# A ScalarE Square with its scale in an engine register, and q's transposes copied by ScalarE instead of VectorE

## The chip, the cores and the metric

The kernel runs on one core of one Trainium2 chip. The metric is the device time of one execution in microseconds (us). Five engines of the core matter here: TensorE (PE in the profile, its weight loads PEld), VectorE (DVE), ScalarE (ACT), GpSimd (POOL) and SyncE (SP), which issues all the DMAs. Each engine executes its own queue in order and waits for the others by semaphores.

## The reference

Two stages. First an attention through 49 agents, for 2 batches of 12480 tokens of width 128; then a feed-forward layer of width 2048 whose activation is a rational function.

```
a2k = softmax(scale * agents @ k.T);  agent_v = a2k @ v          # 49 x 128 per batch
q2a = softmax(scale * q @ agents.T);  x = q2a @ agent_v          # 24960 x 128
h = x @ w_in                                                     # 24960 x 2048
P = a0 + a1*h + a2*h^2 + a3*h^3
Q = 1 + |b0|*|h| + |b1|*h^2
out = (P / (Q + 1e-6)) @ w_out                                   # 24960 x 128
```

## The kernel before

The matrix `agent_v` (49 x 128) is multiplied by `w_in` once per batch, so that h comes directly from the softmax weights of q: h = q2a @ M with M = agent_v @ w_in. M is kept as two parts in fp32r, `m_hi` and `m_lo`.

**Tiling.** Tokens go in 49 blocks of 512; w_in's columns in 16 chunks of 128. A block times a chunk is a 128 x 512 tile of h, and three such tiles in a row make a unit: 784 tiles, 262 units. A unit's h stands in PSUM in one of two slots of three banks. The loop of `main` (lines 595 to 630) makes a step per unit. In step i the engines get, in this order in their queues:

- ACT, `act(i)`: the Square of unit i (line 545, `x = (h + xb)^2`), then, for a pair of earlier units, in turn a Ln (line 559) or an Exp with factor -1 (line 561), which together give 1/Q; then what other streams have put on hold for ACT (`run_hold`).
- DVE: `dve2(i)` (line 574, `w = max(h, mu) + x`, from which the Ln makes the denominator's logarithm), `dve1(i)` (line 566, `u = (x + kap) * h`, over x), its hold list, and for every fourth unit `dve_last` (line 579, `u = (u + om) * w`, for the unit six steps back).
- POOL: for the other three of four units the same product in two instructions: `u = u + om` (line 617) and, six steps later, `u = u * w` (line 612).
- PE, `mm1(i + 1)` (lines 480 and 481: three tiles of h, two matmuls each), `mm2(i - 7)` (line 488: the product with w_out, 16 chunks added up in one of two banks `outb`), and then one piece of another stream (`attend`), which uses the `outb` bank that mm2 doesn't use at the time.

A slot of h is read by the Square, dve2 and dve1, and is free for the unit after next when all three have finished. So every engine's queue order and the two slots together set the pace.

**Streams beside the loop.** `q_stream` makes the softmax of q for every second block: scores (line 209), maximum and difference (408, 409), Exp (413), sum and reciprocal (418, 419), the split in two fp32r parts on POOL (426 to 428), then two sets of four PE transposes (line 433, `q_tr`) and for each set a copy of the 113 x 512 result from PSUM to the tile `pT` (line 439, `q_trev`), which mm1 reads as its moving operand. `a2k_stream` computes batch 1's agent attention in the first half of the loop, `w_stream` decodes the rest of w_out at its start.

**Coefficients.** `coefs` (lines 309 to 387) turns a and b into about forty per-partition columns of the tile `cf`, by small DVE and POOL instructions in the opening stage, before the loop. h is scaled by `rho` so that the formulas above hold; a flag chooses between the loop described here and a slower general one. The prologue (lines 718 to 842) is batch 0's agent attention.

Of the kernel before, what the change touches and what calls it, by code (L numbers as in the profile page):

```python
# [11 lines left out]
F32 = mybir.dt.float32  # L12
F32R = mybir.dt.float32r
I32 = mybir.dt.int32
U32 = mybir.dt.uint32
AF = mybir.ActivationFunctionType
# [6 lines left out]
A = 49  # L23
# [24 lines left out]

MAX_G, MAX_A, MAX_K, MAX_C = 16.0, 8.0, 1e9, 1e3

GAP, LAG = 6, 7

ON_DVE, LAST_DVE = 4, 7
# [9 lines left out]
SUBS = (0, 1, 2, 3)  # L63
SUB_DVE = 5

CO0, COPS = 3, 3
QPE, QTR = 2, 7

WARM, DUM, DUA = 8, 2, 4
# [9 lines left out]
def agent_attention_rational_moe(  # L79
# [24 lines left out]
    ag = const.tile([128, B * A], F32, name="ag")  # L104
    cab = const.tile([128, 6], F32, name="cab")
    b_abs = const.tile([128, 2], F32, name="b_abs")
    cf = const.tile([128, 64], F32, name="cf")
    mcol = const.tile([128, 1], F32, name="mcol")
    flag = const.tile([128, 1], I32, name="flag")
    c0_t = const.tile([128, 1], F32, name="c0_t")  # L110
# [198 lines left out]
    def coefs():  # L309

        ops, at = [], {}

        def later(f, **kw):
            ops.append(lambda: f(**kw))

        def new(nm):
            if nm not in co:
                co[nm] = cf[:, len(co):len(co) + 1]
            return co[nm]

        def ts(nm, x, s1, op0, s2=None, op1=None, eng=DVE):
            kw = {} if op1 is None else {"op1": op1}
            later(eng.tensor_scalar, out=new(nm), in0=x, scalar1=s1, scalar2=s2, op0=op0, **kw)

        def tp(nm, x, s1, op0, s2=1.0, op1=ALU.mult):
            ts(nm, x, s1, op0, s2, op1, POOL)


        big = ("km", "cm", "om", "A0", "K", "rho", "mu")
        for nm in big + tuple(nm + "_" for nm in big):  # L330
            new(nm)
        sizes, signed = cf[:, len(big):2 * len(big)], cf[:, :len(big)]

        mul, add = ALU.mult, ALU.add
        ge, le = ALU.is_ge, ALU.is_le
        mag, fit, safe = (sm_p.tile([128, 6], F32, name=n) for n in ("mag", "fit", "safe"))
        later(DVE.scalar_tensor_tensor, out=mag, in0=cab, scalar=-1.0, in1=cab, op0=mul, op1=ALU.max)
        later(DVE.tensor_scalar, out=fit, in0=mag, scalar1=MAX_C, scalar2=None, op0=le)
        later(DVE.scalar_tensor_tensor, out=fit[:, 3:6], in0=mag[:, 3:6], scalar=1.0 / MAX_C, in1=fit[:, 3:6], op0=ge, op1=mul)
        later(DVE.tensor_reduce, out=new("fits"), in_=fit, axis=AX.X, op=ALU.min)  # L340
        ts("unfit", co["fits"], -1.0, mul, 1.0, add)
        later(DVE.tensor_scalar, out=b_abs, in0=mag[:, 4:6], scalar1=1.0, scalar2=None, op0=mul)
        later(DVE.tensor_scalar, out=safe, in0=cab, scalar1=co["fits"], scalar2=co["unfit"], op0=mul, op1=add)
        later(DVE.tensor_scalar, out=mag, in0=mag, scalar1=co["fits"], scalar2=co["unfit"], op0=mul, op1=add)
        a0, a1, a2, a3 = (safe[:, i:i + 1] for i in range(4))
        b0, b1 = mag[:, 4:5], mag[:, 5:6]
        later(DVE.reciprocal, out=new("r3"), in_=a3)
        later(DVE.reciprocal, out=new("rb0"), in_=b0)
        ts("pos", a2, a3, mul, 0.0, ALU.is_gt)
        ts("sig", co["pos"], -2.0, mul, 1.0, add)  # L350
        tp("bb", b1, co["rb0"], mul, 0.5, mul)
        tp("rho", co["bb"], co["sig"], mul)
        tp("t2", co["rho"], co["r3"], mul)
        tp("A2", a2, co["t2"], mul)
        tp("t1", co["t2"], co["rho"], mul)
        tp("A1", a1, co["t1"], mul)
        tp("t0", co["t1"], co["rho"], mul)
        tp("A0", a0, co["t0"], mul)
        tp("mu", co["A2"], 1.0, mul, 0.5, add)
        tp("c", co["mu"], 0.5, mul, co["A1"], add)  # L360
        tp("kap", co["c"], 1.0, mul, -0.0625, add)
        tp("cm", co["c"], co["mu"], mul)
        tp("om", co["cm"], -1.0, mul, co["A0"], add)
        tp("ig", co["bb"], co["rb0"], mul, 0.5, mul)
        tp("xb", co["mu"], -1.0, mul, -0.25, add)
        tp("mg", co["mu"], 1.0, mul, 0.0625, add)
        tp("lb", co["ig"], C0, mul, co["mg"], ALU.subtract)
        tp("km", co["kap"], co["mu"], mul)
        at["late"] = len(ops)
        later(DVE.reciprocal, out=new("G"), in_=co["ig"])  # L370
        later(DVE.reciprocal, out=new("K"), in_=co["t0"])
        tp("Kg", co["K"], co["ig"], mul)
        later(DVE.scalar_tensor_tensor, out=sizes, in0=signed, scalar=-1.0, in1=signed, op0=mul, op1=ALU.max)
        ts("mu_G", co["mu_"], co["G"], mul)
        ts("ok0", co["mu_G"], MAX_G, le, co["fits"], mul)
        ts("ok1", co["G"], 4 * MAX_G, le, co["ok0"], mul)
        ts("sum", co["km_"], co["cm_"], add, co["om_"], add)
        ts("A0_m", co["A0_"], MAX_A, mul, -0.0625, add)
        ts("ok2", co["sum"], co["A0_m"], le, co["ok1"], mul)
        ts("ok3", co["K_"], MAX_K, le, co["ok2"], mul)  # L380
        ts("ok4", co["rho_"], 1.0 / MAX_C, ge, co["ok3"], mul)
        ts("ok5", co["rho_"], MAX_C, le, co["ok4"], mul)
        later(DVE.tensor_copy, out=flag, in_=co["ok5"])
        ts("bad", co["ok5"], -1.0, mul, 1.0, add)
        ts("rho_s", co["rho"], co["ok5"], mul, co["bad"], add)
        later(DVE.tensor_scalar, out=mcol, in0=ident[:, A:A + 1], scalar1=co["mu"], scalar2=co["ok5"], op0=mul, op1=mul)
        return ops, at["late"]


# [59 lines left out]
    def main(wk, streams, fast):  # L449
# [91 lines left out]
        def act(i):  # L541
            if i < NU:
                h, w, x, y = slot(i), view("w", i), view("x", i), view("u", i)
                if fast:
                    ACT.activation(out=x, in_=h, func=AF.Square, bias=co["xb"])  # L545
                else:
                    ACT.activation(out=x, in_=h, func=AF.Abs)
                    ACT.activation(out=y, in_=h, func=AF.Identity, scale=cab[:, 3:4], bias=cab[:, 2:3])
                    POOL.tensor_scalar(out=w, in0=x, scalar1=b_abs[:, 1:2], scalar2=b_abs[:, 0:1], op0=ALU.mult, op1=ALU.add)
            if fast:  # L550
                p = (i - 3) // 2
                ready = pair(p) if 0 <= p and 2 * p < NU else []
                ln, ex = i % 2 == 1, i % 2 == 0
            else:
                ready = [view("w", i - 1)] if 0 <= i - 1 < NU else []
                ln = ex = True
            for r in ready:
                if ln:
                    ACT.activation(out=r, in_=r, func=AF.Ln, bias=arm["lb"])  # L559
                if ex:  # L560
                    ACT.activation(out=r, in_=r, func=AF.Exp, scale=-1.0)  # L561

        def dve1(i):
            h, x, y = slot(i), view("x", i), view("u", i)
            if fast:
                DVE.scalar_tensor_tensor(out=y, in0=x, scalar=co["kap"], in1=h, op0=ALU.add, op1=ALU.mult)  # L566
            else:
                DVE.tensor_tensor(out=y, in0=h, in1=y, op=ALU.mult)
                DVE.scalar_tensor_tensor(out=y, in0=y, scalar=cab[:, 1:2], in1=h, op0=ALU.add, op1=ALU.mult)

        def dve2(i):
            h, x, w = slot(i), view("x", i), view("w", i)
            if fast:
                DVE.scalar_tensor_tensor(out=w, in0=h, scalar=co["mu"], in1=x, op0=ALU.max, op1=ALU.add)  # L574
            else:
                DVE.tensor_tensor(out=w, in0=w, in1=x, op=ALU.mult)

# [55 lines left out]
    def q_stream(g0):  # L633
        for g in range(g0, NQ):
            yield (g, None, None)
            yield (None, lambda bk: q_pe(g, bk), [("DVE", lambda bk: q_ev(g, bk))])
            if g + 1 < NQ:
                load_q(g + 1)
            yield (None, None, [("ACT", lambda bk: q_exp(g))])
            yield (None, None, [("DVE", lambda bk: q_sum(g))])  # L640
            yield (None, None, [("POOL", lambda bk: q_split(g)[0]())])
            yield (None, None, [("POOL", lambda bk, j=j: q_split(g)[j]()) for j in (1, 2)])
            yield (None, None, [])
            yield ("late", lambda bk: q_tr(g, 0, bk), [("DVE", lambda bk: q_trev(g, 0, bk, DVE.tensor_copy))])
            if q_n(g) > 4:
                yield ("late", lambda bk: q_tr(g, 1, bk), [("DVE", lambda bk: q_trev(g, 1, bk, DVE.tensor_copy))])

    def w_scale(h):
        w = wo.rearrange("p a b -> p (a b)")[:, h * WP:(h + 1) * WP]
# [64 lines left out]
    with tc.manual_schedule():  # L714
# [136 lines left out]
        def rest(fast):  # L851
# [3 lines left out]
            for n, r in rings.items():  # L855
                r[1] = turns.get(n, 0)
            if fast:
                arm.update(om=co["om"], lb=co["lb"])
            else:
                arm.update(om=cab[:, 0:1], lb=c0_t)  # L860
            main(wk, [q_stream(1), w_stream(fast), a2k_stream(kv, 1, G1)], fast)
# [42 lines left out]
```

## Time and profile before

| | |
|---|---|
| three runs | 1279.61, 1290.75, 1291.05 us; median 1290.75 us |
| profiled execution | 1280.74 us; span 1278.9 us, 1.84 us lie around the span |
| granted TensorE clock over the span | 0.994 |
| PE busy | 1214.2 us (95%) |
| DVE busy | 1211.8 us (95%) |
| ACT busy | 1161.1 us (91%) |
| POOL busy | 1151.9 us (90%) |
| Square (line 545) | 262 instructions, 402.2 us |
| copies of q's transposes on DVE (line 439) | 47 instructions, 32.0 us |

A busy time counts each moment once, although the records of successive instructions on one engine overlap a little: an instruction's record ends when its writes are done, and the next one starts a little before. So what an instruction takes from its engine's time is the distance from its start to the start of the next one where that one follows at once, and this is shorter than its record. PE's busy time holds modelled ends and isn't a measure of how much room PE has. The loop begins 66 us after the start of the span; until about 600 us batch 1's attention runs beside it.

### The profile page before, as it was taken

To read this page: it belongs to the slowest core of one execution; us is meant where nothing else is said; L and a number is where in the kernel's file an instruction comes from. 1 tells how busy PE (TensorE), PEld (TensorE's weight loads), DVE (VectorE), ACT (ScalarE), POOL (GpSimd) and SP (SyncE) were. 2 spreads that over 40 slices of the span, in tenths; PEclk is the share of its full clock that TensorE was granted. 3 is DMA by queue.
4 is the path that set the end of the run, shared out by engine and by line. 5 is a ranking of instruction groups with operands and counts; after the bars stand their busy time and mean duration, and the time that the engine had idled before them with its cause. 6 is when DMAs were issued, how large, how long until landed. Compare 5 with 4: busy or idle time off the path is not lost.

```text
span 1278.9 us, 14253 instructions
## 1 busy us (share of the span) xinstructions
PE 1214.2 (95%) x5396; PEld 700.8 (55%) x5396; DVE 1211.8 (95%) x941; ACT 1161.1 (91%) x705; POOL 1151.9 (90%) x535
## 2 busy tenths in 40 slices
PE   7969999999999999999999999999999999999998
PEld 6745555555555555555555555555555555555554
DVE  5899999999999999999999999999999999999996
ACT  3478998999999999999999999999999999999995
POOL 3549999989999999999999999999999999999992
PEclk8999999999999999999999999999999999999999
DMA  9511111111011211210000000000000000000000
GB/s 360 201 45 33 42 59 50 42 58 46 34 42 46 62 50 50 58 38 9 33 9 25 34 24 9 34 25 12 30 25 17 25 26 9 33 15 9 17 9 26
DMA packets 22397, 56.60 MB, mean 44 GB/s; under 512 B 2736, under 2 KB 3248, under 8 KB 22320
## 3 DMA queue, kind: packets, MB, share of 16 engines
q1 hardware_dynamic: 22320, 55.61, 12.8%
q8 instruction: 44, 0.72, 0.2%
q14 instruction: 33, 0.27, 0.1%
HBM read 42.82 MB, written 12.78 MB: 43 GB/s over the span
## 4 chain that ended last, share of the span: by engine, by line
DVE 42%; PE 26%; POOL 15%; ACT 8%; issue 8%; DMA 1%; SPq 0%; POOLq 0%; DVEq 0%; ACTq 0%
DVE w L574 17%; DVE u L566 16%; PE outb L488 14%; POOL u L612 8%; POOL u L617 5%; ACT u L545 5%; PE slot L480 4%; PE slot L481 4%; DVE u L579 2%; ACT w L559 2%; PE outb L209 1%; ACT w L561 1%; DVE pT L439 1%; PE outb L433 1%; DVE qs L418 1%
## 5 line engine op out<-in xcount | busy, mean ns | idle before, releaser
L488 PE MATMUL outb<-u,wo 128*128 128x512 f32 (+1 forms) x1568 | 716.7, 593 | 19.8 <-POOL u L612 13.3
L612 POOL TENSOR_TENSOR u<-u,w 128x1536 f32<-128x1536 f32 x192 | 689.4, 3603 | 0.0
L574 DVE SCALAR_TENSOR_TENSOR w<-slot,cf,u 128x1536 f32<-128x1536 f32 (+1 forms) x262 | 471.0, 1798 | 25.5 <-ACT u L545 23.7
L566 DVE SCALAR_TENSOR_TENSOR u<-u,cf,slot 128x1536 f32<-128x1536 f32 (+1 forms) x262 | 472.3, 1803 | 9.3
L488 PEld LDWEIGHTS outb<-u,wo 128*128 128x128 f32 x1568 | 292.1, 189 | 308.3 <-issue 242.1
L545 ACT ACTIVATE u<-slot,cf 128x1536 f32<-128x1536 f32 (+1 forms) x262 | 402.2, 1536 | 62.0 <-PE slot L481 28.1
L617 POOL TENSOR_SCALAR u<-u,cf 128x1536 f32<-128x1536 f32 x192 | 368.3, 1920 | 59.1 <-DVE u L566 58.8
L480 PE MATMUL slot<-pT,m_hi 113*128 113x512 f32 (+3 forms) x800 | 362.7, 455 | 21.5 <-DVE u L566 21.4
L559 ACT ACTIVATE w<-w,cf 128x3072 f32<-128x3072 f32 (+1 forms) x134 | 373.2, 2788 | 0.0
L561 ACT ACTIVATE w<-w 128x3072 f32<-128x3072 f32 (+1 forms) x134 | 361.0, 2696 | 0.0
L481 PE MATMUL slot<-pT,m_lo 113*128 113x512 f32 (+3 forms) x800 | 311.4, 390 | 0.0
L480 PEld LDWEIGHTS slot<-pT,m_hi 113*128 113x128 f32 x800 | 150.3, 188 | 108.5 <-DVE u L566 64.1
L481 PEld LDWEIGHTS slot<-pT,m_lo 113*128 113x128 f32 x800 | 151.0, 189 | 42.8 <-issue 17.8
L579 DVE SCALAR_TENSOR_TENSOR u<-u,cf,w 128x1536 f32<-128x1536 f32 (+1 forms) x70 | 142.3, 2039 | 0.0
L433 PEld LDWEIGHTS outb<-ident,p 128*113 128x113 f32 x187 | 26.4, 178 | 28.3 <-issue 20.3
L209 PEld LDWEIGHTS outb<-ag,q 128*64 128x64 f32 x748 | 23.8, 138 | 17.8 <-issue 12.5
L439 DVE CAST pT<-outb 113x512 fp32r<-113x512 f32 (+1 forms) x47 | 32.0, 681 | 0.0
L433 PE MATMUL outb<-ident,p 128*113 128x128 f32 x187 | 28.5, 275 | 3.6 <-DVE o L496 1.6
L496 ACT COPY o<-outb 128x512 f32<-128x512 f32 (+1 forms) x40 | 23.0, 574 | 9.0 <-PE outb L488 9.0
L181 POOL TENSOR_TENSOR r<-r,s 128x512 f32<-128x512 f32 x6 | 9.2, 1534 | 21.8 <-DVE s L178 21.8
L209 PE MATMUL outb<-ag,q 128*64 128x49 f32 x748 | 26.8, 224 | 0.0
L428 POOL TENSOR_TENSOR p<-e,p 128x392 fp32r<-128x392 f32 (+1 forms) x25 | 23.9, 955 | 2.1
(135 smaller groups left out, 447.8 us busy)
## 6 DMA issues: line engine op xcount, KB each, us to landing
q<-qT SPq DMA_DIRECT2D x24, 512.0 KB, 3.5
outT<-o SPq DMA_DIRECT2D x48, 256.0 KB, 2.0
v<-vP SPq DMA_DIRECT2D x24, 258.0 KB, 2.7
k<-kT SPq DMA_DIRECT2D x24, 256.0 KB, 2.7
v<-vP SPq DMA_DIRECT2D x9, 645.0 KB, 11.7
k<-kT SPq DMA_DIRECT2D x8, 640.0 KB, 9.0
raw<-w_in SPq DMA_DIRECT2D x4, 512.0 KB, 11.7
raw<-w_out SPq DMA_DIRECT2D x2, 512.0 KB, 10.4
```

What stands on the lines that cost most here:

```text
L433: PE.transpose(bank[:KR, c * CH:(c + 1) * CH], t[:, h * 4 + c, :].bitcast(F32), ident[:CH, :CH])
L480: PE.matmul(s[:, j, lo:hi], lhsT=m_hi[b][:KR, f], rhs=rhs, start=True, stop=False)
L481: PE.matmul(s[:, j, lo:hi], lhsT=m_lo[b][:KR, f], rhs=rhs, start=False, stop=True)
L488: PE.matmul(outs[blk % 2][:, :width(blk)], lhsT=wo[:, fc, :], rhs=g[:, j, :], start=fc == 0, stop=fc == NFC - 1)
L545: ACT.activation(out=x, in_=h, func=AF.Square, bias=co["xb"])
L559: ACT.activation(out=r, in_=r, func=AF.Ln, bias=arm["lb"])
L561: ACT.activation(out=r, in_=r, func=AF.Exp, scale=-1.0)
L566: DVE.scalar_tensor_tensor(out=y, in0=x, scalar=co["kap"], in1=h, op0=ALU.add, op1=ALU.mult)
L574: DVE.scalar_tensor_tensor(out=w, in0=h, scalar=co["mu"], in1=x, op0=ALU.max, op1=ALU.add)
L579: DVE.scalar_tensor_tensor(out=view("u", u), in0=view("u", u), scalar=arm["om"], in1=view("w", u), op0=ALU.add, op1=ALU.mult)
L612: POOL.tensor_tensor(out=view("u", g), in0=view("u", g), in1=view("w", g), op=ALU.mult)
L617: POOL.tensor_scalar(out=y, in0=y, scalar1=1.0, scalar2=arm["om"], op0=ALU.mult, op1=ALU.add)
```

## The change

Two things are changed.

The Square now computes `(xb * h' + 1)^2`, where xb is an ACT register and the 1.0 an immediate of the instruction; before, it computed `(h + xb)^2` with xb read from the tile `cf` as a per-partition bias. For that h' = h / xb^2, so that the whole is the old one divided by xb^2. The other coefficients of the loop (kap, mu, lb, om and rho) are scaled by `lam` = 1/xb^2 to fit, and the factor on w_out by xb^2. The register is loaded from `cf` once, at the head of the loop's branch. `coefs` has ten small instructions more (three on DVE, seven on POOL, among them those that choose the sign of `rho` by another rule), and its last part is spread over the opening stage four at a time instead of three.

The 47 copies of q's transposes in the loop go from DVE's hold list to ACT's: `q_trev` calls `ACT.copy` in place of `DVE.tensor_copy`.

```diff
-CO0, COPS = 3, 3
+CO0, COPS = 3, 4
...
-        ts("sig", co["pos"], -2.0, mul, 1.0, add)
+        ts("side", co["pos"], 2.0, mul, -1.0, add)
         tp("bb", b1, co["rb0"], mul, 0.5, mul)
-        tp("rho", co["bb"], co["sig"], mul)
+        tp("br", co["bb"], co["r3"], mul, co["side"], mul)
+        ts("near", co["br"], a2, mul, NEAR, le)
+        ts("sig", co["near"], -2.0, mul, 1.0, add)
+        tp("rho", co["bb"], co["sig"], mul, co["side"], mul)
...
+        tp("x2", co["xb"], co["xb"], mul)
...
-        tp("Kg", co["K"], co["ig"], mul)
+        tp("Kg", co["K"], co["ig"], mul, co["x2"], mul)
+        later(DVE.reciprocal, out=new("lam"), in_=co["x2"])
+        tp("kap_l", co["kap"], co["lam"], mul)
+        tp("mu_l", co["mu"], co["lam"], mul)
+        tp("lb_l", co["lb"], co["lam"], mul)
+        tp("om_l", co["om"], co["lam"], mul, co["lam"], mul)
+        tp("rho_l", co["rho"], co["lam"], mul)
...
-                    ACT.activation(out=x, in_=h, func=AF.Square, bias=co["xb"])
+                    ACT.activation(out=x, in_=h, func=AF.Square, scale=arm["xb"], bias=1.0)
...
-                DVE.scalar_tensor_tensor(out=y, in0=x, scalar=co["kap"], in1=h, op0=ALU.add, op1=ALU.mult)
+                DVE.scalar_tensor_tensor(out=y, in0=x, scalar=co["kap_l"], in1=h, op0=ALU.add, op1=ALU.mult)
...
-            yield ("late", lambda bk: q_tr(g, 0, bk), [("DVE", lambda bk: q_trev(g, 0, bk, DVE.tensor_copy))])
+            yield ("late", lambda bk: q_tr(g, 0, bk), [("ACT", lambda bk: q_trev(g, 0, bk, ACT.copy))])
             if q_n(g) > 4:
-                yield ("late", lambda bk: q_tr(g, 1, bk), [("DVE", lambda bk: q_trev(g, 1, bk, DVE.tensor_copy))])
+                yield ("late", lambda bk: q_tr(g, 1, bk), [("ACT", lambda bk: q_trev(g, 1, bk, ACT.copy))])
...
+                xb = ACT.alloc_register("xb")
+                ACT.reg_load(xb, co["xb"][0:1, :].bitcast(I32))
+                arm.update(om=co["om_l"], lb=co["lb_l"], xb=xb)
```

Line numbers behind the coefficients are 12 higher in the changed kernel: the Square is on line 557, dve2 on 586, dve1 on 578, dve_last on 591, the copies on 451, the Ln and Exp on 571 and 573.

DVE's queue at the first two copies of the loop, before (`pT` is the copied transposes, `outb` the bank that PE wrote, `slot` h, `u` and `w` the units' tiles):

```order
L574 SCALAR_TENSOR_TENSOR w_745<-slot_712,cf,u_743 128x1536
L566 SCALAR_TENSOR_TENSOR u_743<-u_743,cf,slot_712 128x1536
L439 CAST pT_930<-outb_68 113x512
L574 SCALAR_TENSOR_TENSOR w_745<-slot_713,cf,u_744 128x1536
L566 SCALAR_TENSOR_TENSOR u_744<-u_744,cf,slot_713 128x1536
L439 CAST pT_930<-outb_68 113x512
L579 SCALAR_TENSOR_TENSOR u_738<-u_738,cf,w_746 128x1536
L574 SCALAR_TENSOR_TENSOR w_746<-slot_712,cf,u_735 128x1536
```

On DVE a copy stood behind dve1 and ahead of dve_last or of the next step's dve2; in the changed kernel these rows follow each other without it.

ACT's queue at the same steps in the changed kernel:

```order
L557 ACTIVATE u_754<-slot_722 128x1536
L573 ACTIVATE w_758<-w_758 128x3072
L451 CAST pT_939<-outb_68 113x512
L557 ACTIVATE u_755<-slot_723 128x1536
L571 ACTIVATE w_759<-w_759,cf 128x3072
L451 CAST pT_939<-outb_68 113x512
L557 ACTIVATE u_746<-slot_722 128x1536
L573 ACTIVATE w_759<-w_759 128x3072
```

A copy now stands behind a step's Ln or Exp and ahead of the next step's Square, and the Square no longer has `cf` among its sources.

ACT's queue at the head of the loop's branch in the changed kernel:

```order
L294 COPY avt<-bank_104 128x49
L877 TENSOR_LOAD flag
L878 COMPARE_AND_BRANCH
L871 TENSOR_LOAD cf
L301 ACTIVATE m_hi_87<-outb_67,mcol 113x512
```

The second TENSOR_LOAD, of xb into the register, is new and stands ahead of the first rounding of M.

## Rows read from the trace of the kernel before

**Rows 1.** Page, part 1: busy time (share of span) and instructions by engine.

```profile
PE 1214.2 (95%) x5396; PEld 700.8 (55%) x5396; DVE 1211.8 (95%) x941; ACT 1161.1 (91%) x705; POOL 1151.9 (90%) x535
```

**Rows 2.** Windows, two stretches: length, then busy time (instructions) of PE, PEld, DVE, ACT, POOL; clock, DMA.

```profile
100.00:600.00 500.00, 486.43 (x2266) 274.91 (x2265) 478.67 (x368) 468.19 (x292) 472.53 (x217) 1.00 0.15 46
650.00:1250.00 600.00, 576.70 (x2116) 324.52 (x2115) 586.93 (x386) 577.73 (x302) 582.44 (x239) 1.00 0.06 21
```

**Rows 3.** Chain that ended last, by line: the page for the span, then from 650 to 1250.

```profile
DVE w L574 17%; DVE u L566 16%; PE outb L488 14%; POOL u L612 8%; POOL u L617 5%; ACT u L545 5%; PE slot L480 4%; PE slot L481 4%; DVE u L579 2%; ACT w L559 2%; PE outb L209 1%; ACT w L561 1%; DVE pT L439 1%; PE outb L433 1%; DVE qs L418 1%
...
by line: DVE w L574 22.1%; DVE u L566 20.5%; issue 10.4%; POOL u L612 10.0%; PE outb L488 7.7%; POOL u L617 5.9%; ACT u L545 5.2%; DVE u L579 3.2%; PE slot L480 2.7%; PE slot L481 2.5%; ACT w L559 2.3%; ACT w L561 1.4%; DVE pT L439 1.0%; PO
```

**Rows 4.** Windows of single lines, 650 to 1250: the Squares, then the copies (DVE, ACT).

```profile
650.00:1250.00 600.00, 209.02 (x136) 1.00 0.06 21
...
650.00:1250.00 600.00, 16.97 (x25) 0.00 (x0) 1.00 0.06 21
```

**Rows 5.** Line 439, by engine: duration minimum/median/maximum in ns; below, who waited (us, times).

```profile
L439 DVE CAST pT<-outb x47: 551/684/686, 106.5 to 1221.2; 113x512 fp32r<-113x512 f32 x46, 113x384 fp32r<-113x384 f32 x1
L439 ACT CAST pT<-bank x2: 561/568/575, 53.4 to 53.9; 113x512 fp32r<-113x512 f32 x2
...
  PEld outb L209: 3.8, 5
  PEld outb L267: 3.3, 3
```

**Rows 6.** Timeline of DVE around one copy: start, length, engine, line, operation.

```profile
700.64 0.68 DVE L439 CAST pT<-outb 113x512 fp32r<-113x512 f32 x1
701.24 1.81 DVE L574 SCALAR_TENSOR_TENSOR w<-slot,cf,u 128x1536 f32<-128x1536 f32 x1
```

**Rows 7.** Timeline of ACT in the prologue (two copies merged) and in the loop.

```profile
53.39 1.04 ACT L439 CAST pT<-bank 113x512 fp32r<-113x512 f32 x2
...
722.16 1.53 ACT L545 ACTIVATE u<-slot,cf 128x1536 f32<-128x1536 f32 x1
723.59 2.77 ACT L561 ACTIVATE w<-w 128x3072 f32<-128x3072 f32 x1
```

**Rows 8.** Lines by shape: count, busy, mean ns of one, idle time before and its releasers.

```profile
L545 ACT ACTIVATE u<-slot,cf 128x1536 f32<-128x1536 f32 x256 | 395.6, 1546 | 60.0 <-PE slot L481 26.4 <-issue 15.9 <-POOL u L617 7.7
L559 ACT ACTIVATE w<-w,cf 128x3072 f32<-128x3072 f32 x128 | 366.7, 2865 | 0.0
L561 ACT ACTIVATE w<-w 128x3072 f32<-128x3072 f32 x128 | 355.0, 2773 | 0.0
```

**Rows 9.** POOL's line 617, min/median/max ns; a timeline piece where DVE's line 579 meets them.

```profile
L617 POOL TENSOR_SCALAR u<-u,cf x192: 1536/1560/3192, 71.4 to 1238.9; 128x1536 f32<-128x1536 f32 x192
...
748.29 4.59 POOL L617 TENSOR_SCALAR u<-u,cf 128x1536 f32<-128x1536 f32 x2
...
748.58 2.87 DVE L579 SCALAR_TENSOR_TENSOR u<-u,cf,w 128x1536 f32<-128x1536 f32 x1
```

**Rows 10.** Timeline of POOL while the DVE copy that starts at 700.64 runs.

```profile
699.99 6.92 POOL L612 TENSOR_TENSOR u<-u,w 128x1536 f32<-128x1536 f32 x2
```

**Rows 11.** Waits, 650 to 1250: who for whom, us in total, times, longest.

```profile
POOL u L617 <- DVE u L566: 16.3, 21, 2.7
...
DVE w L574 <- ACT u L545: 6.6, 19, 0.7
```

**Rows 12.** Line 863 on ACT, and ACT's timeline behind the branch.

```profile
L863 ACTq TENSOR_LOAD <-flag x1: 461/461/461, 58.4 to 58.4; - x1
...
60.67 0.69 ACT L299 ACTIVATE m_hi<-outb,mcol 113x512 fp32r<-113x512 f32 x1 [2.09 <-PE outb L296]
...
65.81 1.55 ACT L545 ACTIVATE u<-slot,cf 128x1536 f32<-128x1536 f32 x1 [0.75 <-DMA u<-w_out]
```

**Rows 13.** Timeline of DVE behind the first coefficients.

```profile
7.73 0.72 DVE L191 TENSOR_REDUCE rows<-bank 128x49 f32<-128x245 f32 x2
10.82 0.41 DVE L191 TENSOR_REDUCE rows<-bank 128x49 f32<-128x245 f32 x1 [2.36 <-ACT S L222]
```

More of the change, by code (lines that the diff above doesn't have):

```diff
@@ L49 @@
 MAX_G, MAX_A, MAX_K, MAX_C = 16.0, 8.0, 1e9, 1e3
+NEAR = 0.375
 GAP, LAG = 6, 7
@@ L106, in agent_attention_rational_moe @@
     b_abs = const.tile([128, 2], F32, name="b_abs")
-    cf = const.tile([128, 64], F32, name="cf")
+    cf = const.tile([128, 96], F32, name="cf")
     mcol = const.tile([128, 1], F32, name="mcol")
@@ L384, in coefs @@
         ts("bad", co["ok5"], -1.0, mul, 1.0, add)
-        ts("rho_s", co["rho"], co["ok5"], mul, co["bad"], add)
-        later(DVE.tensor_scalar, out=mcol, in0=ident[:, A:A + 1], scalar1=co["mu"], scalar2=co["ok5"], op0=mul, op1=mul)
+        ts("rho_s", co["rho_l"], co["ok5"], mul, co["bad"], add)
+        later(DVE.tensor_scalar, out=mcol, in0=ident[:, A:A + 1], scalar1=co["mu_l"], scalar2=co["ok5"], op0=mul, op1=mul)
         return ops, at["late"]
@@ L573, in dve2 @@
             if fast:
-                DVE.scalar_tensor_tensor(out=w, in0=h, scalar=co["mu"], in1=x, op0=ALU.max, op1=ALU.add)
+                DVE.scalar_tensor_tensor(out=w, in0=h, scalar=co["mu_l"], in1=x, op0=ALU.max, op1=ALU.add)
             else:
@@ L857, in rest @@
             if fast:
-                arm.update(om=co["om"], lb=co["lb"])
+                xb = ACT.alloc_register("xb")
+                ACT.reg_load(xb, co["xb"][0:1, :].bitcast(I32))
+                arm.update(om=co["om_l"], lb=co["lb_l"], xb=xb)
             else:
```

## The prediction

> **What bounds the kernel now.** First the busy times [rows 1]: PE and DVE stand at 95%, ACT at 91%, POOL at 90%. These are means over a prologue and a loop, so the next view is two stretches inside the loop [rows 2]. From 650 to 1250 us, where only q's softmax runs beside the loop, DVE is busy 586.9 of 600 us (97.8%), POOL 582.4 (97.1%), ACT 577.7 (96.3%); PE's 576.7 holds modelled ends. From 100 to 600 the three stand at 95.7, 94.5 and 93.6%. So the reader is to see four engines nearly full, DVE the fullest. Third, the chain that ended last [rows 3]: DVE's two lines of each unit hold 33% of the span, PE's large matmuls 22%, POOL's two lines 13%, the Square 5%; the copies that the change moves hold 1%. From 650 to 1250 the same copies hold 1.0%, 6.0 us. A unit takes 600 / 136 = 4.41 us there [rows 4].
>
> **The change, part by part.**
>
> *The copies leave DVE.* One takes 0.60 us of DVE's time: the next instruction starts at 701.24, the copy at 700.64 [rows 6]; its record of 684 ns [rows 5] overlaps the next. 47 copies make 28.2 us, the 25 of the late stretch [rows 4] 15.0 us. On the chain are only 6.0 us of those 15.0 [rows 3]; for 47 copies that is 6.0 x 47 / 25 = 11.3 us. The rest lies beside PE or POOL work that was as late.
>
> *The copies come to ACT.* The same copy stands in the trace on ACT, twice, in the prologue: 568 ns as a record [rows 5], two of them 1.04 us [rows 7], so 1.04 - 0.575 = 0.47 us of the engine's time. 47 make 22.1 us, 25 make 11.8 us. A copy stands behind a step's Ln or Exp and delays the next Square by up to 0.47 us. Behind that Square wait dve2 and dve1, and behind these PE's mm1 for the same slot. DVE waits for Squares 6.6 us in 600 already [rows 11].
>
> *The Square loses its per-partition bias.* The trace has no ACTIVATE with a register as an operand, so the price is bounded. The Ln reads a bias from `cf`, the Exp of the same shape reads only immediates, and they differ by 2865 - 2773 = 92 ns [rows 8]; so the Square is at best 0.092 us shorter, 24.1 us over 262 of them and 12.5 us over the 136 of the late stretch. Nothing in the trace excludes a loss: neighbours on ACT overlap by 0.10 us (a Square's record is 1.53 us, the next starts 1.43 us behind it [rows 7]), and if the register has to be read in between, that overlap could be lost. So the ends are -0.092 and +0.10 us per Square. I take -0.092, since the Exp, which reads no tile for scale or bias, is the nearest row: the new Square reads none either, and a queue of instructions of 1.4 to 2.8 us leaves much time to make the next one ready.
>
> *Loads after.* In the 600 us: DVE 586.9 - 15.0 = 571.9; ACT 577.7 + 11.8 - 12.5 = 577.0; POOL stays at 582.4 and is the fullest. POOL's stay is not an accident: when DVE's fourth-unit product (line 579, two SBUF inputs) meets a POOL instruction, one of them stands still. In [rows 9] two of line 617 take 4.59 us, where the median of one is 1.56, and line 579 takes 2.87. The change leaves all that. If the fullest engine can again be kept 97.8% busy, the 600 us become 582.4 / 0.978 = 595.5, so 4.5 us less, and over the loop's 1213 us (from 65.8, [rows 12]) 9.1 us.
>
> *By the chain.* The copies give 11.3. Squares hold 5% of the span, 64 us or 45 of them at 1.43 us, and 45 x 0.092 = 4.1. The copies on ACT come back with ACT's share of the chain, 5.2 + 2.3 + 1.4 = 8.9% [rows 3]: 22.1 x 0.089 = 2.0. Sum 11.3 + 4.1 - 2.0 = 13.4 us, if nothing else is as late. Since POOL is, I take **10 us**, near the first way.
>
> *Costed at nothing.* The register's load: the flag's took 461 ns on ACT [rows 12]; ACT idles 2.09 us before the first rounding of M, and the first Square waits 0.75 us for w_out's DMA, so even a late rounding is hidden. Without that DMA wait it would cost 0.5 us. The ten coefficient instructions: DVE waits 2.36 us behind its second row maximum [rows 13], and POOL is idle there; two more exchanges between DVE and POOL fit in. PE gets q's scores and transposes into `outb` as before; it waited 7.1 us for DVE's copies [rows 5] and will wait for ACT's, which end at about the same point of the step. No DMA, no instruction of POOL's loop and none of PE's is moved.
>
> *A rule on the copies.* While the DVE copy of [rows 6] ran, POOL's two products took 6.92 us, 3.46 each [rows 10], so such a copy doesn't hold POOL up. The Trainium skill (SBUF — State Buffer, Who interferes with whom) says that a VectorE cast can take the port pair that it shares with GpSimd, and that GpSimd then stands still for the whole instruction. Were that so here, each copy moved would free POOL of 0.60 us too, and the gain would be nearer to 28 us. The trace does not agree for this copy. The same section says that a VectorE instruction with two SBUF inputs does collide with GpSimd's reads; rows 9 agree with that.
>
> **The sum.** 1280.74 (profiled execution) - 10 = 1270.7 us. The three runs have a median of 1290.75, 10 us above that execution; the four times make two pairs, near 1280 and near 1291, and the page of one of them doesn't tell what parts them. From the median the sum is 1280.8. I take the middle, **1276 us**, and measure the rivals from the same middle of before, 1286.
>
> **The rivals.**
>
> 1. *Taken up.* POOL and ACT are within 1.5% of DVE, and ACT's copies come in lumps ahead of a Square. For it: the first stretch's chain is shared by four engines and only 1% of the chain is copies. Against it: DVE holds 17 + 16 + 2% of the chain. Gain 0 to 4 us, 1284 us.
>
> 2. *The whole saving.* DVE sets the pace everywhere, and the 28.2 us of its copies come off, with a few us of Square waits. For it: 97.8%. Against it: 6.0 of 15.0 us on the chain. Gain 17 to 28 us, about 1263 us. The Trainium skill (Perfetto Trace Analysis, Optimization Strategy) has it that the engine with the highest occupancy is the one whose relief pays; by it alone all of DVE's saving would show. The chain's rows bear out less than half.
>
> 3. *Slower: ACT becomes the bound.* Place: the Square's operand. Price: with no saving per Square ACT's load is 577.7 + 11.8 = 589.5, at 97.8% filling 602.8 us per 600, so 5.6 us more over the loop; at +0.10 us per Square it is 603.1 and 616.7, so 34 us more. It decides from a saving below 0.02 us per Square on ((586.9 - 577.7 - 11.8) / 136). Middle of it: +20 us, 1306 us. For it: no row shows such an operand, and ACT has only 3.7% left. Against it: the engine's arithmetic is the same.
>
> 4. *It doesn't do what it says.* A new sign rule or flag could send the work to the general loop. With the reference's a and b, `br` times a2 is 0.158, below 0.375, `rho` keeps its value of -0.611, and the flag's terms are those of before. Left at 0.02.
>
> **Chances and range.** Forecast (gain 4 to 17 us) 0.51; taken up 0.20; whole saving 0.12; slower 0.15; not what it says 0.02. About 1%, 12.8 us, is what a measurement of this kernel can tell from no change. Of the forecast 0.22 lies beyond it, so faster 0.34; slower is rival 3's upper part and rival 4, 0.12; the rest, 0.54, within 1%. The range goes from 1261 (20 us below the profiled execution, into rival 2) to 1297 (the median and rival 3's lower end).
>
> **What would show it.** The Square's mean at 1454 ns and a start-to-start of 1.34 us; at 1546 or more rival 3. Copies on ACT at 568 ns, none on DVE in the loop. From 650 to 1250 DVE's share at about 96%, POOL's up to 98 or 99% and the most Squares per us; DVE's waits for the Square no longer than 6.6 us. If ACT's share goes beyond 98% and dve2's waits for the Square double, the copies' lumps decide and rival 1 or 3 holds. If DVE stays fullest per unit and the unit falls below 4.33 us, it is rival 2. The prediction is wrong if a Square costs more with the register, or if POOL's stalls by line 579 grow as DVE and POOL fall into another step.

## The result and the profile after

The changed kernel takes 1276.16 us (median of 12 runs, 1274.78 to 1277.01), the kernel before in the same series 1290.05 us (12 runs, 1279.61 to 1296.22). The ratio is 0.9912 with a 95% interval of 0.9889 to 0.9935: faster by 0.9%, and at 1276 us, as forecast. The sum behind it is another matter: the two profiled executions differ by 6.0 us only, and the runs before lie in two groups. Two of the 12 are at 1280 us, nine at 1288 to 1291, one at 1296; those of the changed kernel are all within 2.3 us. So the 13.9 us between the medians are about 4 us between the lower groups (1280.0 to 1276.2) and about 10 us that come because the changed kernel never came out in the upper group. The 0.9% is mostly a matter of the groups; what the change does to the loop is 0.4%, as shown below.

Page, part 1 (busy time and its share of the span by engine), which answers to [rows 1]:

```profile
PE 1213.9 (95%) x5396; PEld 702.1 (55%) x5396; DVE 1187.1 (93%) x897; ACT 1157.7 (91%) x752; POOL 1154.5 (91%) x542
```

DVE lost 24.7 us and 44 instructions net, ACT lost 3.4 us in all although it has 47 more, POOL has the seven coefficients. The two stretches of [rows 2], after:

```profile
100.00:600.00 500.00, 488.80 (x2272) 276.53 (x2273) 468.96 (x349) 470.13 (x314) 475.22 (x218) 1.00 0.15 46
650.00:1250.00 600.00, 577.85 (x2122) 325.82 (x2121) 576.73 (x363) 576.48 (x328) 584.31 (x239) 1.00 0.06 21
```

In the late stretch POOL is now the fullest, 97.4%; DVE and ACT stand at 96.1%. The lines themselves, by shape, against [rows 8] and [rows 5] (count, busy, mean ns, idle time before and its releasers):

```profile
L557 ACT ACTIVATE u<-slot 128x1536 f32<-128x1536 f32 x256 | 373.5, 1460 | 57.2 <-PE slot L493 25.8 <-issue 13.3 <-POOL u L629 10.0
L586 DVE SCALAR_TENSOR_TENSOR w<-slot,cf,u 128x1536 f32<-128x1536 f32 x256 | 463.4, 1810 | 45.6 <-ACT u L557 40.3 <-POOL u L629 2.2 <-DMA k<-kT 1.5
L451 ACT CAST pT<-outb 113x512 fp32r<-113x512 f32 x46 | 27.2, 592 | 0.3 <-PE outb L445 0.3
```

The Square takes 1460 ns in place of 1546, without its operand from `cf`; the copies take 592 ns on ACT. DVE now idles 40.3 us before dve2 for the Square. ACT's timeline shows the distance from a Square's start to the next instruction's, 1.33 us (1.43 in [rows 7]):

```profile
721.78 1.45 ACT L557 ACTIVATE u<-slot 128x1536 f32<-128x1536 f32 x1
723.11 2.88 ACT L571 ACTIVATE w<-w,cf 128x3072 f32<-128x3072 f32 x1
```

The chain that ended last, by line, first the page, then 650 to 1250 (against [rows 3]):

```profile
PE outb L500 13%; DVE w L586 13%; POOL u L624 13%; DVE u L578 11%; POOL u L629 9%; ACT u L557 7%; PE slot L492 4%; PE slot L493 4%; ACT w L571 2%; DVE u L591 1%; DMA k<-kT 1%; PE outb L211 1%; ACT w L573 1%; PE outb L445 1%; POOL p L440 1%
...
by line: POOL u L624 16.2%; DVE w L586 15.6%; DVE u L578 12.6%; POOL u L629 10.8%; issue 10.6%; PE outb L500 9.0%; ACT u L557 8.0%; PE slot L492 2.7%; PE slot L493 2.5%; ACT w L571 2.4%; DVE u L591 1.9%; POOL p L440 1.0%; PE outb L445 0.9%;
```

DVE's two lines went from 42.6% of the late stretch to 28.2%, POOL's from 15.9 to 27.0, and the copies are no longer among the lines listed, on either engine.

To keep the loop apart from prologue and tail I use one measure below, **the way**: from the start of the first Square to that of the 251st. Its two ends are rows of ACT's timeline; the first of the kernel before is 65.81 [rows 12]. Before, then after:

```profile
1210.71 1.53 ACT L545 ACTIVATE u<-slot,cf 128x1536 f32<-128x1536 f32 x1
```

```profile
64.77 1.46 ACT L557 ACTIVATE u<-slot 128x1536 f32<-128x1536 f32 x1 [0.77 <-DMA u<-w_out]
...
1204.76 1.45 ACT L557 ACTIVATE u<-slot 128x1536 f32<-128x1536 f32 x1
```

So the way went from 1144.9 to 1140.0 us, 4.9 us or 0.4% shorter. Each way below is read from one execution, too. Experiments 7 to 10 leave this part of the loop as it is and tell how far it repeats: 1145.0 and 1145.0 us for the kernel before, 1140.8 and 1140.2 for the changed one. So the 4.9 us are clear, and differences under 1 us say nothing. One more us is the earlier first Square, which is at 63.5 to 65.9 us in all kernels of this study without an order to it.

**The two groups.** Near the end POOL has no line 617 left to do and runs four products of line 612 in a row, and in this stretch DVE does the product of unit 251 (line 579, two SBUF inputs). Timelines of POOL and DVE there: the kernel before (an execution of the lower group), the changed kernel, and the kernel before with the copies moved alone (first experiment; an execution of the upper group):

```profile
1240.44 15.27 POOL L612 TENSOR_TENSOR u<-u,w 128x1536 f32<-128x1536 f32 x4
...
1244.15 4.81 DVE L579 SCALAR_TENSOR_TENSOR u<-u,cf,w 128x1536 f32<-128x1536 f32 x1
```

```profile
1234.49 15.29 POOL L624 TENSOR_TENSOR u<-u,w 128x1536 f32<-128x1536 f32 x4
...
1238.02 4.99 DVE L591 SCALAR_TENSOR_TENSOR u<-u,cf,w 128x1536 f32<-128x1536 f32 x1
```

```profile
1242.30 13.68 POOL L612 TENSOR_TENSOR u<-u,w 128x1536 f32<-128x1536 f32 x4
...
1246.00 11.60 DVE L579 SCALAR_TENSOR_TENSOR u<-u,cf,w 128x1536 f32<-128x1536 f32 x1
```

Alone, this product takes 1.81 us. In the first two it waits for the rest of one POOL product, gets in between, and the next POOL product is the one that is held up (15.3 us for four). In the third POOL's four run through at 3.42 us each, and DVE stands still until the last is done, with dve2 and dve1 of the following steps behind it: 6.8 us more for this product, and from the 251st Square to the end of the span it is 76.8 us there against 68.2 in the other two. The traces of the other experiments agree. Two more executions are of an upper group: in experiment 3 this product takes 11.61 us and the stretch behind the 251st Square 76.8, in experiment 4 it waits for two POOL products:

```profile
1237.24 8.42 DVE L594 SCALAR_TENSOR_TENSOR u<-u,cf,w 128x1536 f32<-128x1536 f32 x1
```

There the stretch is 74.2 us. In the executions of experiments 2 and 5 to 8, all of a lower group, the product takes 4.8 to 5.0 us and the stretch 68.1 to 68.4.

### The profile page after: what moved, and what is told of

The parts are those of the page before. It is cut to its first block, busy times and chain, and to the rows that moved or that the text cites. A ratio compares the mean times of both kernels' runs of the same rounds, so it can differ in the third digit from the quotient of the medians.

```text
span 1273.0 us, 14264 instructions
## 1 busy us (share of the span) xinstructions
PE 1213.9 (95%) x5396; PEld 702.1 (55%) x5396; DVE 1187.1 (93%) x897; ACT 1157.7 (91%) x752; POOL 1154.5 (91%) x542
## 4 chain that ended last, share of the span: by engine, by line
DVE 31%; PE 24%; POOL 23%; ACT 11%; issue 9%; DMA 1%; SPq 0%; POOLq 0%; DVEq 0%; ACTq 0%
PE outb L500 13%; DVE w L586 13%; POOL u L624 13%; DVE u L578 11%; POOL u L629 9%; ACT u L557 7%; PE slot L492 4%; PE slot L493 4%; ACT w L571 2%; DVE u L591 1%; DMA k<-kT 1%; PE outb L211 1%; ACT w L573 1%; PE outb L445 1%; POOL p L440 1%
## 5 line engine op out<-in xcount | busy, mean ns | idle before, releaser
L586 DVE SCALAR_TENSOR_TENSOR w<-slot,cf,u 128x1536 f32<-128x1536 f32 (+1 forms) x262 | 471.0, 1798 | 45.6 <-ACT u L557 40.3
L557 ACT ACTIVATE u<-slot 128x1536 f32<-128x1536 f32 (+1 forms) x262 | 379.7, 1450 | 59.7 <-PE slot L493 27.8
L492 PE MATMUL slot<-pT,m_hi 113*128 113x512 f32 (+3 forms) x800 | 366.6, 460 | 18.3 <-DVE u L578 17.7
L451 ACT CAST pT<-outb 113x512 fp32r<-113x512 f32 (+1 forms) x47 | 27.7, 590 | 0.3 <-PE outb L445 0.3
## 6 DMA issues: line engine op xcount, KB each, us to landing
raw<-w_in SPq DMA_DIRECT2D x4, 512.0 KB, 11.3
raw<-w_out SPq DMA_DIRECT2D x2, 512.0 KB, 11.3
```

Source lines behind the costliest of these rows:

```text
L492: PE.matmul(s[:, j, lo:hi], lhsT=m_hi[b][:KR, f], rhs=rhs, start=True, stop=False)
L557: ACT.activation(out=x, in_=h, func=AF.Square, scale=arm["xb"], bias=1.0)
L586: DVE.scalar_tensor_tensor(out=w, in0=h, scalar=co["mu_l"], in1=x, op0=ALU.max, op1=ALU.add)
```

## The experiments

All were timed beside runs of the kernel before. There the kernel before was in the lower group (1278 to 1282 us) in 57 of 86 runs, in the series of the result in 2 of 12. So medians of different series, and medians within one, can differ by the groups alone, and the way is the better measure of the loop.

**1. The copies alone**, on the kernel before:

```diff
-            yield ("late", lambda bk: q_tr(g, 0, bk), [("DVE", lambda bk: q_trev(g, 0, bk, DVE.tensor_copy))])
+            yield ("late", lambda bk: q_tr(g, 0, bk), [("ACT", lambda bk: q_trev(g, 0, bk, ACT.copy))])
...
```

The second set's line is changed in the same way.

> The kernel before with the 47 copies moved to ScalarE, the Square as it was. Theory A (load: the fullest engine sets the pace at 97.8% busy): ScalarE gets 22 us more and nothing back, its load from 650 to 1250 is 589 of 600, so about 5 us slower than the kernel before, 1283 to 1300 us, and ScalarE busy 98% there. Theory B (VectorE's time is what counts, ScalarE has room): most of the gain of the whole change is here, 8 to 14 us faster than before.

Measured: 1285.85 us, ratio 1.0025 (0.9996 to 1.0055), 7 runs at 1284 to 1287 and 5 at 1288 to 1294; the lowest run is 1284.10 where the kernel before reaches 1277.89. The interval of the ratio reaches 1; the way is 1149.1 us (from 63.52), 4.2 longer than before, and that is clear. The 251st Square, and the late stretch, with ACT at 586.9 of 600 us:

```profile
1212.58 1.54 ACT L545 ACTIVATE u<-slot,cf 128x1536 f32<-128x1536 f32 x1
...
650.00:1250.00 600.00, 577.19 (x2116) 324.40 (x2114) 571.21 (x360) 586.94 (x326) 580.97 (x240) 1.00 0.06 21
```

Theory A holds: in the late stretch DVE is busy 15.7 us less, the loop is slower, and ACT has become the fullest engine.

**2. The Square alone**, on the changed kernel, the two lines of the first experiment turned back.

> The changed kernel with the copies back on VectorE: only the Square with its scale in the register. The Square's mean is 1454 to 1460 ns. Theory A (load): VectorE stays the fullest with its copies, so only the Squares on the chain pay, 0 to 5 us faster than before. Theory B (the way from Square to dve2 sets the pace): 24 us less on ScalarE and an earlier VectorE, 10 us or more faster than before.

Measured: 1278.44 us, ratio 0.9981 (0.9951 to 1.0012); 7 runs at 1277 to 1279 and 5 at 1284.7 to 1287.0; Square 1453 ns; the way 1141.8 us, 3.1 less than before. DVE is the fullest in the late stretch, 589.6 of 600 us. Theory A. The two halves don't add up: +4.2 alone and -3.1 alone, but -4.9 together. What the copies cost depends on whether ACT has the time, and the shorter Square makes it.

**3. The scale from the tile:**

```diff
-                    ACT.activation(out=x, in_=h, func=AF.Square, scale=arm["xb"], bias=1.0)
+                    ACT.activation(out=x, in_=h, func=AF.Square, scale=co["xb"], bias=1.0)
```

> The changed kernel with the scale read from the tile of coefficients instead of the register, bias 1.0 as in the change. Theory A (what made the Square shorter is that it reads no per-partition operand): the Square is 1546 ns again, and the time is that of the copies moved alone. Theory B (a bias costs, a scale doesn't): the Square stays at 1455 ns and the time at 1276 us.

Measured: 1288.09 us, ratio 1.0039 (1.0008 to 1.0070), 6 runs at 1283 to 1286 and 6 at 1290 to 1296. The Square is back at 1549 ns, and the way is 1149.1 us, that of the copies alone to the tenth:

```profile
L557 ACT ACTIVATE u<-slot,cf 128x1536 f32<-128x1536 f32 x256 | 396.5, 1549 | 42.4 <-PE slot L493 21.4 <-POOL u L629 6.8 <-issue 6.6
```

Theory A: a per-partition operand costs the 0.09 us, as bias or as scale, and the register doesn't. The rescaling of h is only the means to it.

**4. No copies on any engine:**

```diff
+        if g > 0:
+            pT_t[g] = pT_t[0]
+            return
         if h == 0:
```

> The changed kernel without the 47 copies in the loop on any engine; mm1 reads the first group's transposes for all blocks, the PE transposes stay. Takes 22 us off ScalarE. Theory A (POOL is the fullest now, 97.4%): 0 to 4 us faster than the changed kernel, 1272 to 1276 us. Theory B (the copies' lumps ahead of the Square cost what the DVE waits for the Square grew by, 24.2 us in all of which 8 in the late stretch): 8 to 15 us faster, 1261 to 1268 us.

Measured: 1281.50 us (1272.81 to 1283.59, and one run at 1292.92; ratio 0.9973, 0.9944 to 1.0002), more often in an upper group, here 8 us higher; the median misses both theories, and the lowest run is 1272.81. The way is 1138.3 us, 1.7 less than the changed kernel's. Theory A for the loop. DVE still waits for the Square as long as in the changed kernel (650 to 1250; us in all, times, longest; the changed kernel first):

```profile
DVE w L586 <- ACT u L557: 15.0, 33, 1.4
...
DVE w L589 <- ACT u L560: 15.6, 33, 1.4
```

So the doubled wait isn't the copies' doing. It is room: DVE has less to do and comes to the Square earlier. With the copies back on DVE (second experiment) it was 4.0 us, with DVE relieved further (sixth) 22.7.

**5. POOL with 21 us less.** The third instruction of q's split is left out in the loop.

```diff
-            yield (None, None, [("POOL", lambda bk, j=j: q_split(g)[j]()) for j in (1, 2)])
+            yield (None, None, [("POOL", lambda bk, j=j: q_split(g)[j]()) for j in (1,)])
```

> The changed kernel without the third instruction of q's split (POOL, 0.93 us of its time for each of 23 groups: 21 us), so p2's low part is stale. Theory A (after the change POOL is the fullest and sets the pace): the way from the first Square to the 251st falls from 1140.0 by 6 us or more, against 1.7 us when ScalarE got 22 us less. Theory B (no engine alone sets it, the chain goes round through all): 0 to 3 us.

Measured: 1265.88 us, ratio 0.9873 (0.9830 to 0.9917), one of the 6 runs at 1274.79. The way is 1129.9 us (from 65.53), 10.1 less than the changed kernel's:

```profile
1195.44 1.45 ACT L557 ACTIVATE u<-slot 128x1536 f32<-128x1536 f32 x1
```

Theory A. POOL's busy time fell by 22.5 us (1154.5 to 1132.0), so it is 0.45 us for each us (0.48 by the 21 us of the plan). Part of it may be fewer meetings of the two engines: DVE's 64 whole products of line 591 take 133.2 us in all, in the changed kernel 136.7.

**6. VectorE with 17 us less.** q's sum and reciprocal are left out in the loop.

```diff
+        if g > 0:
+            s_t[g] = ones[:, :n].unsqueeze(2)
+            return
         s = ring(sm_p, 2, [CH, QG, 1], F32, "qs")[:, :n, :]
```

> The changed kernel without q's sum and reciprocal in the loop (DVE, 0.72 us for each of 23 groups: 17 us); POOL multiplies by a constant tile. Theory A (POOL is the fullest, VectorE has room since the change): the way from the first Square to the 251st falls by 0 to 2 us. Theory B (VectorE still sets the pace): by 6 us or more.

Measured: 1270.49 us, ratio 0.9896 (0.9857 to 0.9934); the way 1135.3 us, 4.7 less. Between the two theories: DVE's busy time fell by 13.7 us (1187.1 to 1173.4), so 0.34 us for each us (0.28 by the 17 us of the plan). So POOL's being the fullest doesn't mean that only POOL counts.

**7 and 8. The last step's product later**, in the kernel before and in the changed one:

```diff
-            if i == NU - 1:
-                dve_last(fin.pop())
```

> The kernel before with one thing moved: in the last step with a Square the product of the last pair unit on VectorE (line 579) no longer stands ahead of dve2 and dve1 but behind them. Theory A (the kernel before has two times 9 us apart because that product, at 1244 to 1246 us, stands still behind one or behind three POOL products in a row): it comes 3.6 us later, holds nobody up for long, and the runs lie in one group within 3 us, near 1280 us. Theory B (the two times come from elsewhere, the prologue's clock or DMA): two groups 9 us apart as before.

> The changed kernel with the same move of the last step's product. Theory A: the changed kernel's product waited behind one POOL product only (4.9 us in place of 1.8), so 0 to 4 us faster than the changed kernel's 1276 us, one group. Theory B: no difference, 1276 us.

Measured: 1281.53 us, ratio 1.0004 (0.9973 to 1.0035), 7 runs at 1279.6 to 1281.6 and 5 at 1287.7 to 1290.4; and 1276.65 us, ratio 0.9966 (0.9936 to 0.9996), 9 runs at 1275.2 to 1277.2 and 3 at 1283.3 to 1285.6. Both missed: this moves the product of unit 255, and the one that stands still is unit 251's, four steps earlier. They say nothing on the cause. But the second shows that the changed kernel isn't proof against the upper group: it is the same program up to the last step with a Square.

**9 and 10. Unit 251's product to POOL, unit 254's to VectorE**, in the kernel before and in the changed one:

```diff
-        return u % ON_DVE != ON_DVE - 1 and u < NU - LAST_DVE
+        return (u % ON_DVE != ON_DVE - 1 or u == 251) and u < NU - LAST_DVE and u != 254
...
-            a = (i, i, -1, i - 1)[i % ON_DVE]
+            for a in ((i, i, -1, i - 1)[i % ON_DVE],) + ((251,) if i == 252 else ()):
```

> The kernel before with two products of the tail exchanged: unit 251's goes from VectorE to POOL and unit 254's from POOL to VectorE. Theory A (the two groups of times of the kernel before, 9 us apart, come from unit 251's product on VectorE, which waits for one POOL product, 4.8 us, or for three in a row, 11.6 us): all runs lie in one group within 3 us, at 1276 to 1281 us, and no product on VectorE takes over 6 us before 1250 us. Theory B (the groups come from elsewhere): two groups 8 to 9 us apart.

> The changed kernel with the same exchange. Theory A: it was already in the short group in 12 of 12 runs, so only the stall of 3.2 us goes: 1272 to 1276 us, one group. Theory B: 1276 us and no difference.

Measured, ninth: 1281.41 us (11 runs, 1279.36 to 1283.49), ratio 0.9985 (0.9964 to 1.0007); the kernel before beside it had 9 of 28 runs at 1286 to 1292. One group, 4.1 us wide where 3 were expected: theory A holds for the kernel before. Tenth: 1275.59 us, ratio 0.9951 (0.9925 to 0.9977), 11 runs at 1274.0 to 1277.5, one at 1286.39. DVE has no long product there; POOL runs six in a row and DVE waits a little for the Square instead:

```profile
1228.98 20.68 POOL L624 TENSOR_TENSOR u<-u,w 128x1536 f32<-128x1536 f32 x6
...
1237.66 1.42 DVE L586 SCALAR_TENSOR_TENSOR w<-slot,cf,u 128x1152 f32<-128x1152 f32 x1 [1.07 <-ACT u L557]
```

So the 3.2 us did not come off: from the 251st Square to the end it is 67.7 us against 68.2, which is theory B. What the one run of 1286 met isn't known. 1275.59 isn't clear of the changed kernel's 1276.16, which was timed in another series.

**11 and 12. q's rounding off POOL**, on top of the tenth, to VectorE and to ScalarE:

```diff
-            yield (None, None, [("POOL", lambda bk, j=j: q_split(g)[j]()) for j in (1, 2)])
+            yield (None, None, [("DVE", lambda bk: q_split(g)[1](DVE))])
+            yield (None, None, [("POOL", lambda bk: q_split(g)[2]())])
...
```

This is the eleventh; in the twelfth `ACT.copy` does the rounding at the same place.

> The changed kernel with that exchange, and with q's rounding (second instruction of the split, 0.6 us of POOL for each of 23 groups, 14 us) on VectorE, a step earlier. Theory A (an us taken off POOL gave 0.48, one off VectorE 0.28): 3 to 5 us faster than the exchange alone, unless the copy from SBUF to SBUF on VectorE holds POOL up. Theory B (all engines are even, moving work gives nothing): within 1 us of the exchange alone.

> The same with the rounding on ScalarE, 0.42 us each, 10 us. Theory A (22 us off ScalarE gave only 1.7, so ScalarE has room): 4 to 6 us faster than the exchange alone, the fastest of all, 1267 to 1271 us. Theory B (ScalarE with 10 us more becomes the fullest, as when the copies came without the shorter Square): no gain or slower.

Measured: 1294.24 us, ratio 1.0098 (1.0059 to 1.0137), the way 1158.3 us; and 1278.35 us, ratio 0.9975 (0.9947 to 1.0004), the way 1141.9, 1.7 more than the tenth's 1140.2. On VectorE the rounding (392 elements per partition, SBUF to SBUF) collides with POOL, min/median/max in ns:

```profile
L439 DVE TENSOR_SCALAR p<-e x24: 255/1590/3840, 99.2 to 1225.8; 128x392 fp32r<-128x392 f32 x23, 128x147 fp32r<-128x147 f32 x1
```

The 255 is the last one, of 147 elements; the shortest of 392 takes 354 ns. The rounding makes 37.3 us of DVE records, and POOL's busy time falls by 10.6 us only (1153.0 to 1142.4). On ScalarE it costs 518 ns each and POOL's load falls, but ACT's rises to 579.2 of 600 us, and the way grows: the outcome of theory B. The load alone doesn't explain it, since ACT at 96.5% is less full than POOL was in the tenth (97.3%). What grew is waiting: in the late stretch POOL waits 24.1 us for dve1 against 13.5 in the tenth, and DVE's 64 whole products of line 591 take 140.1 us in all against 134.0. Why they meet POOL's more often isn't shown. No version of this study is clearly faster than the changed kernel and computes all of it.

## Why the prediction was right, and where not

- **The Square's price** was right: 92 ns foretold, 1546 to 1460 measured, 24.1 us foretold for all, 22.5 measured (402.2 to 379.7). Experiment 3 shows that the operand makes it, and the register takes next to nothing of it back.
- **The copies' prices** were right: 24.7 us off DVE with three more coefficients on it (28.2 foretold), 592 ns each on ACT (568 in the prologue). Against experiment 2, which differs in the copies alone, they take 25.9 us off DVE's busy time and put 19.6 on ACT's (22.1 foretold). ACT's load hardly moved, 577.7 to 576.5.
- **"Loads after"** was right as a ranking (POOL first) and too large as a time. It took the fullest engine to be kept 97.8% busy again; POOL is kept 97.4%, and the way became 4.9 us shorter where 9.1 stood. Experiments 4 to 6 show why one engine's share isn't the time: an us of busy time less on POOL gives 0.45, on DVE 0.34, on ACT 0.09 (1.7 of 19.5 us), and in experiment 5 the fullest of the three is at 97.0% in the late stretch, and the loop is shorter. Rival 2's rule on the engine with the highest occupancy stands in the Trainium skill (Perfetto Trace Analysis, Identifying the Most-Contended Engine); here DVE, the fullest, lost 24.7 us and the loop 4.9.
- **"By the chain"** failed: it priced the copies at 11.3 - 2.0 = 9.3 us of gain, and alone they lose 4.2 us. The chain says what was late, not what would be late next, and it priced ACT's part by ACT's share of the chain, while what counts is how little ACT has left. The load way gave 5.6 us slower for the same case (rival 3 without a saving): 4.2 measured.
- **The sum** of 10 us was 6.0 between the two profiled executions, of which 4.9 in the loop: the lower end of the forecast's own 4 to 17 us, at the edge of rival 1. The load way alone was the better of the two ways, and still too high.
- **The base of the sum.** I found two pairs of times and took the middle without a cause. A hint was in the trace, unit 251's product at 4.81 us; the long stall shows only in the upper executions traced later. That 1276 came out is luck: a gain taken too large was subtracted from a middle at which the kernel before hardly ever runs. From 1280.7 the sum is 1270.7, and the changed kernel lies at 1276.
- **What would show it.** DVE's share came as said (96%); POOL's rose to 97.4, not to 98 or 99. "DVE's waits for the Square no longer than 6.6 us" was wrong: 15.0, and by experiment 4 that is no sign of the copies' lumps. The stalls of line 579 hardly grew: its 64 whole products take 135.0 us before and 136.7 after.
- **Nothing for the register's load and the coefficients** held: the load took 286 ns, and the first Square still waited 0.77 us for w_out's DMA.

Shown: the operand's price, that the copies pay only where ACT has room for them, that POOL's and DVE's load both count and ACT's hardly does in the changed kernel, the cause of the two groups in the kernel before. Open: why the changed kernel met the upper group in none of 12 runs. Its sibling (experiment 8) did in 3 of 12, so it may be chance. What decides which of the two gets in isn't known: unit 251's product comes 3.5 to 3.7 us behind the start of POOL's row of four in all three timelines above, and nearly the same distance goes with either outcome, 3.71 us with 4.81 and 3.70 with 11.60. Open too: the upper runs of experiments 10 and 12 (1 and 3 of 12), where that product isn't on DVE.

## What to carry to other kernels

When four engines are 95 to 98% busy, price a move by what the receiving engine has left: moved work that fits costs little (1.7 us for 47 copies), and the same work on an engine at 96% without relief made the loop 4.2 us longer. So pair such a move with a saving on the receiver, as here, and test both halves alone. Where run times come in two groups, look in the trace for the one instruction that takes several times its median before explaining a difference of medians.

## What the runs showed of the hardware

- A VectorE instruction with two SBUF inputs can stand still behind more than one GpSimd instruction: 11.60 us for one of 1.81, while four POOL products ran back to back; in other executions of like code it got in earlier (8.42 and 4.81). The Trainium skill (SBUF — State Buffer, Who interferes with whom) says that the one that comes second stands still until the first has finished; here it can be passed over several times.
- The copy from PSUM on VectorE didn't collide with POOL (none of the 47 took over 686 ns [rows 5]; POOL beside one of them, [rows 10]), the rounding from SBUF to SBUF of 392 elements did (median 1590 ns, the shortest 354). The same section says of copies and casts that they can contend, under conditions on their operands; here the second did and the first did not.
- An ACTIVATE whose scale is an engine register is 89 ns shorter than one with the scale in SBUF: 1460 ns against 1549, both with an immediate bias.
